# Sums of folded weights by VectorE in SBUF instead of adding transfers through DRAM, and a new early order with the first two weight tiles in halves

## The chip, the core and the metric

One core of a Trainium2 chip runs the whole program. The metric is the device time of one execution in microseconds (us), the median over runs. TensorE (PE) multiplies, VectorE (DVE) and ScalarE (ACT) convert and evacuate, GpSimd (POOL) copies small things, SyncE (SP) issues nearly all transfers. PEld is TensorE's loading of stationary operands.

## The reference

Attention with a local window and block summaries, and a bilinear feed-forward layer on its output. The shapes: 4 batches, 8 heads, 768 positions of 64; weights 512 x 1024 (w1, w2), 1024 x 1024 (w3), 1024 x 512 (w_out), all float32.

```python
k_sum = k.reshape(B, H, nb, block, D).max(axis=3)
v_sum = v.reshape(B, H, nb, block, D).mean(axis=3)
scores_l = scale * np.matmul(q, k.transpose(0, 1, 3, 2))
mask_l = np.abs(pos[:, None] - pos[None, :]) < window
scores_s = scale * np.einsum('bhsd,bhnd->bhsn', q, k_sum) + np.log(block)
a = softmax(np.concatenate([np.where(mask_l, scores_l, -1e9), scores_s], axis=-1))
x = np.matmul(a, np.concatenate([v, v_sum], axis=2))
...
a = x @ w1
b = x @ w2
h = a * b @ w3
return (h @ w_out).astype(np.float32)
```

## The kernel before, in words

**Numbers.** A float32 is carried as two words, a high one that TensorE's fast format holds exactly and a low one, the rest. A product is three matmuls: high x high, low x high, high x low.

**Fold.** Since nothing stands between `w3` and `w_out`, the kernel first computes `wp` = w3 x w_out, eight tiles `wp[0]` to `wp[7]` of 128 x 2 x 512 (two words). The weights arrive in tiles of 1 MB, numbered n = 0 to 19 (n = 0 is the first of `w_out`, 1 the first of `w3`, 12 to 19 are w1 and w2), in raw 64-bit words. `load_weight` issues the load of tile n, `convert` turns it into two words in four steps (the actions `a`, `b`, `c`, `d`): a pass of ScalarE (L203), a shift of VectorE (L228), a cast of ScalarE to the high word (L233) with an OR of VectorE (L235), and VectorE's low word (L161). Where `LAST_BITS` has an A, the last bits come from a second pass of ScalarE (L211) and one OR of VectorE (L219). The first four tiles are converted in two halves. TensorE needs, for its first matmul, half of the `w_out` tile and half of the `w3` tile.

**Order.** In the first part SP and TensorE follow `PLAN`, a list of actions written out by hand: `wN` loads tile N, `aN` to `dN` convert it, `kN` loads keys, `fN` queries, `rN` rows of values, `vN` values, `qN eN xN nN tN oN` are the six pieces of attention step N (scores, exponentials, normalization, transposes, outputs), `RN` gives TensorE N x 100 columns of matmuls. A scheduler places ScalarE's and VectorE's work between. From step 8 on `lump(p)` does the same in code: it writes down step p's scores, then the outputs of step p-2, and runs matmuls between.

**Network.** The first 1024 tokens (u = 0, 1) go through the network in the plain way. The other 2048 (n = 1, 2) use a scheme of seven products in place of eight (`lanes`): `gates` has four row blocks r, of seven products k each, and 24 large matmuls a product and pair of stationary tiles `ws`; `project_fast` follows with `wp`. The scheme needs sums and differences of blocks of the stationary matrices, which are made once on the chip by `stationary`: it forms sums in a tile `wr`, then for each of k = 2, 5, 4, 3 casts the high word (`sp`, ScalarE L673), takes the low word (VectorE), and stores `sp` to DRAM (`wS` for w1 and w2, `pS` for `wp`). `ws` are loaded back from there, six in flight, by `flow_in`. `tend` takes one step of this background work now and then, as matmuls are written down.

**The sums of wp.** `stationary` needs the float32 value of `wp`, high plus low. Before, `spill_high` (action `h`) stores the eight high words to DRAM (`pR`), `join_wp` adds the eight low words to it by adding transfers of GpSimd's queue (one or two beside each of steps 8 to 11), and `sums_of_output` loads `pR` into four tiles `wr` from step 16 (c = 0) and step 18 (c = 1) on. Its `sp` take tiles with the tag `wp`, that of the gate weights tiles with the tag `x` (six buffers, shared with `ws`). The gate weights' sums (`sums_of_gates`) are made in SBUF by VectorE (L918), in a tile with the tag `ring`.

Of the kernel before, what the change touches and what calls it, by code (L numbers as in the profile page):

```python
# [32 lines left out]
f0 w5 R62
w6 b3 a4 R15
c3 w7 d2 d3 R62
R30
a5 b5 r2 r0 a6 f1 b4 K0 F0 c4 d4 c5 v0 b6 q0 d5 c6 R107
w8 M k1 k3 e0 a7 k2 b7 w9 x0 R31
d6 R62
c7 f2 R47  # L40
a8 n0 v1 K1 K2 d7 b8 R31
N w10 L2 F1 w11 L4 c8 t0 a9 q1 d8 V0 F2 b9 R92
e1 o0 c9 d9 v2 a10 q2 R92
R31
x1 w12 f3 L1 a11 V2 K3 L0 S0 f5 L3 F3 n1 V1 t1 b10 e2 b11 x2 S4 R47
f4 c10 w13 d10 S1 o1 n2 a12 v3 R92
b12 c12 t2 c11 q3 L5 d11 F4 w14 o2 e3 S3 a13 b13 d12 a14 b14 w15 x3 n3 L6 w16 w17 V3 c13 v4 a15 f6 S5 a16 d13
S6 c14 R78
d14 b15 f7 b16 S2 c15 c16 d15 w18 a17 w19 b17 W1 L7 v5 V5 a18 c17 d16 d17 R62
b18 a19 b19 c19 c18 d18 t3 q4 R31  # L50
d19 o3 P1 V4 F5 e4 R77
p0 x4 q5 R46
e5 R108
x5 R29
p1 R61
W2 p2 n4 S7 p3 R123
W0 R154
n5 p4 p5 R15
p6 p7 h0 h1 R154
# [3 lines left out]
W3 R62
R76
h7 x6 R107
x7 V6 R92
R77
v7 V7 f8 R62
n6 n7 R32
# [43 lines left out]
def attention_moe(ctx, tc, qG, kW, kT, vP, vW, vB, mask, w1, w2, w3T, wo, out, outT):  # L113
# [545 lines left out]
    def stationary(name, load, to_dram, home, apart=False):  # L659


        if apart:
            t = [[sb.tile([P, 512], F32, name="wr", tag="pt", bufs=6) for _ in range(2)] for _ in range(2)]
        else:
            whole = sb.tile([P, 2, 2, 512], F32, name="wr", tag="ring", bufs=RING)
            t = [[whole[:, i, j] for j in range(2)] for i in range(2)]
# [423 lines left out]
    def budget(columns):  # L1090
# [53 lines left out]
    EXTRA.setdefault(16, []).append(lambda: background.append(sums_of_output(0)))  # L1144
    EXTRA.setdefault(18, []).append(lambda: background.append(sums_of_output(1)))

    for i in range(NF):
        EXTRA.setdefault(8 + i // 2, []).append(lambda i=i: join_wp(i))

# [110 lines left out]
```

## Time and profile before

| | |
|---|---|
| median of 3 runs | 515.13 us (513.4 to 515.14) |
| the profiled execution | 514.52 us |
| its span in the trace | 512.8 us |
| TensorE busy | 487.9 us (95%) |
| VectorE, ScalarE, GpSimd busy | 362.1, 324.1, 48.1 us |
| mean granted TensorE clock | 0.989 of full |
| moved by the DMA engines | 142.95 MB, 279 GB/s |

Busy time is a share of the span for each engine by itself; the engines overlap. All times within the trace are counted from the start of its span. "idle before <-X" names the instruction or transfer whose end released the waiting one.

### The profile page before, as it was taken

To read this page: it belongs to the slowest core of one execution; us is meant where nothing else is said; L and a number is where in the kernel's file an instruction comes from. 1 tells how busy PE (TensorE), PEld (TensorE's weight loads), DVE (VectorE), ACT (ScalarE), POOL (GpSimd) and SP (SyncE) were. 2 spreads that over 40 slices of the span, in tenths; PEclk is the share of its full clock that TensorE was granted. 3 is DMA by queue.
4 is the path that set the end of the run, shared out by engine and by line. 5 is a ranking of instruction groups with operands and counts; after the bars stand their busy time and mean duration, and the time that the engine had idled before them with its cause. 6 is when DMAs were issued, how large, how long until landed. Compare 5 with 4: busy or idle time off the path is not lost.

```text
span 512.8 us, 10326 instructions
## 1 busy us (share of the span) xinstructions
PE 487.9 (95%) x3744; PEld 392.0 (76%) x3744; DVE 362.1 (71%) x877; ACT 324.1 (63%) x888; POOL 48.1 (9%) x86
## 2 busy tenths in 40 slices
PE   0989999999999999999969999999999999999996
PEld 0767777888887777777757888778788888888885
DVE  4898978798825788945279676789978029229972
ACT  5888988884618678877777576747875421423710
POOL 1023311230331111000000000000000000000000
PEclk9989999999999999999979999999999999999999
DMA  8999599995998998999876869985858755656752
GB/s 343 418 404 394 184 366 411 402 408 175 377 263 244 311 295 274 308 363 362 278 287 225 304 234 359 341 271 192 252 164 262 230 185 195 203 176 198 211 199 84
DMA packets 54915, 142.95 MB, mean 279 GB/s; under 512 B 5456, under 2 KB 18256, under 8 KB 52304
## 3 DMA queue, kind: packets, MB, share of 16 engines
q1 hardware_dynamic: 52560, 138.09, 76.6%
q0 software_dynamic: 1152, 2.10, 3.2%
q10 hardware_dynamic: 1152, 2.10, 1.1%
q8 instruction: 30, 0.49, 0.4%
q14 instruction: 21, 0.17, 0.1%
HBM read 109.56 MB, written 32.70 MB: 277 GB/s over the span
## 4 chain that ended last, share of the span: by engine, by line
PE 82%; DMA 8%; ACT 4%; DVE 4%; issue 1%; SPq 0%; DVEq 0%; ACTq 0%
PE ln L719 44%; PE mm L165 27%; PE po L473 4%; PE sc L395 4%; PE tp L453 2%; DMA wraw<-in_wo_dram 2%; DMA wS<-sp 2%; DMA wraw<-in_w_dram 1%; DMA wraw<-in_w3T_dram 1%; DMA wr<-pR 1%; ACT sm L433 1%; ACT wf L203 1%; PE means L322 1%; ACT w L233 1%; ACT wraw L211 0%
## 5 line engine op out<-in xcount | busy, mean ns | idle before, releaser
L719 PE MATMUL ln<-xT,ws 128*128 128x512 f32 x672 | 158.7, 396 | 0.0
L719 PEld LDWEIGHTS ln<-xT,ws 128*128 128x128 f32 x672 | 126.3, 190 | 28.0 <-issue 0.8
L165 PE MATMUL mm<-x,w 128*128 128x512 f32 x384 | 92.0, 395 | 0.9 <-ACT g L542 0.9
L165 PEld LDWEIGHTS mm<-x,w 128*128 128x128 f32 x384 | 70.9, 188 | 17.9 <-ACT g L542 1.3
L423 ACT ACTIVATE sm<-sm,mx 128x120 f32<-128x120 f32 x192 | 73.8, 388 | 7.9 <-DVE mx L409 7.9
L719 PE MATMUL ln<-hT,ws 128*128 128x512 f32 x336 | 78.3, 392 | 0.0
L719 PEld LDWEIGHTS ln<-hT,ws 128*128 128x128 f32 x336 | 62.6, 188 | 13.3 <-DVE hT L161 0.2
L739 DVE TENSOR_TENSOR tmp<-ln,tmp 128x512 f32<-128x512 f32 x52 | 35.7, 687 | 51.0 <-PE ln L719 36.7
L165 PE MATMUL mm<-w,w 128*128 128x512 f32 x192 | 48.8, 409 | 14.5 <-ACT w L233 11.6
L637 ACT CAST hT<-hr 128x512 fp32r<-128x512 f32 x56 | 32.1, 620 | 42.9 <-DVE hr L796 35.3
L165 PEld LDWEIGHTS mm<-w,w 128*128 128x128 f32 x192 | 36.4, 194 | 24.0 <-ACT w L233 11.6
L409 DVE CUSTOM_DVE_ANT_0 sm<-sc,mask_sb 128x120 f32<-128x120 f32 x192 | 42.4, 276 | 7.6 <-PE sc L395 7.5
L165 PE MATMUL mm<-wp,h 128*128 128x512 f32 x192 | 46.0, 394 | 0.0
L433 ACT ACTIVATE sm<-sm,mx 128x120 f32<-128x120 f32 x128 | 38.7, 385 | 8.2 <-DVE mx L429 8.1
L165 PEld LDWEIGHTS mm<-wp,h 128*128 128x128 f32 x192 | 35.5, 188 | 8.0 <-issue 0.5
L161 DVE TENSOR_TENSOR hT<-hr,hT 128x512 fp32r<-128x512 f32 x56 | 35.5, 684 | 4.6 <-ACT hT L637 4.4
L423 ACT ACTIVATION_READ_ACCUMULATOR sm<-sm,mx 128x1 f32 x192 | 36.7, 191 | 0.0
L473 PEld LDWEIGHTS po<-pt,v 120*64 120x64 f32 x768 | 25.4, 141 | 13.4 <-ACT pt L460 4.3
L473 PE MATMUL po<-pt,v 120*64 120x64 f32 x768 | 29.0, 229 | 5.2 <-ACT pt L460 4.1
L382 POOL COPY k<-ks 128x96 f32<-128x96 f32 (+1 forms) x32 | 12.0, 390 | 197.5 <-DMA k<-in_kW_dram 135.1
L161 DVE TENSOR_TENSOR xT<-xraw,xT 128x512 fp32r<-128x512 f32 x28 | 18.7, 684 | 13.0 <-ACT xT L637 13.0
L203 ACT ACTIVATE wf<-wraw 128x1024 f32<-128x1024 f32 (+1 forms) x24 | 23.4, 991 | 6.6 <-DMA wraw<-in_wo_dram 4.8
(63 smaller groups left out, 560.3 us busy)
## 6 DMA issues: line engine op xcount, KB each, us to landing
ws<-wS SPq DMA_DIRECT2D x56, 512.0 KB
v<-in_vW_dram SPq DMA_DIRECT2D x24, 512.0 KB
wraw<-in_w3T_dram SPq DMA_DIRECT2D x8, 1024.0 KB
wraw<-in_w_dram SPq DMA_DIRECT2D x8, 1024.0 KB
wS<-sp SPq DMA_DIRECT2D x16, 512.0 KB
ws<-pS SPq DMA_DIRECT2D x16, 512.0 KB
k<-in_kW_dram SPq DMA_DIRECT2D x20, 368.0 KB
raw<-in_kT_dram SPq DMA_DIRECT2D x16, 392.0 KB
```

What stands on the lines that cost most here:

```text
L161: eng.tensor_tensor(dst, src, hi.bitcast(F32), ALU.subtract)
L165: nc.tensor.matmul(acc, lhsT=a, rhs=b, start=first and i == 0, stop=last and i == len(terms) - 1)
L203: nc.scalar.activation(f[:, some], words[:, some, 1].bitcast(F32), AF.Prelu, scale=2.0**-112, alpha=-(2.0**32),)
L382: nc.gpsimd.tensor_copy(k[:, blocks, CUT : CUT + NB], ks[b, p].unsqueeze(1).broadcast_to([P, n, NB]))
L395: nc.tensor.matmul(sc[h][64 * g : 64 * g + 64, i * KR : (i + 1) * KR], lhsT=q[rows, i * P + 64 * g : i * P + 64 * g + 64], rhs=k[rows, i, ...
L409: nc.vector.tensor_tensor_reduce(out=sm[:, j], in0=sc[h][:, i * KR : (i + 1) * KR], in1=mask_sb[:, 0 if blk == 0 else 2 if blk == BLOCKS - ...
L423: nc.scalar.activation(sm[:, j], sm[:, j], AF.Exp, bias=mx[:, 0, j : j + 1], scale=-1.0, accum_out=mx[:, 1, j : j + 1])
L433: nc.scalar.activation(sm[:, j], sm[:, j], AF.Copy, scale=mx[:, 2, j : j + 1])
L473: nc.tensor.matmul(po[cols, at : at + 64], lhsT=v[:KR, g, i, cols], rhs=pt[g][:, (h * NBLK + i) * 64 : (h * NBLK + i + 1) * 64], start=Tru ...
L637: nc.scalar.copy(dst[0], src)
L719: nc.tensor.matmul(banks[i][:, :U], lhsT=x, rhs=y, start=c + j == 0 and k in o.first, stop=c == steps - 1 and j == 2 and k in o.last, skip ...
L739: nc.vector.tensor_tensor(parts[to], got, parts[more], ALU.add)
```

## The change

The sums of `wp` are made by VectorE: `sums_of_output` adds the two words of `wp` tiles straight into one tile `wr` of the tag `ring`, four adds of 128 x 512 for each c. The DRAM tensor `pR`, `spill_high`, `join_wp` and the loads are gone. Both of its works are appended to the background behind those of the gate weights (action `G`), and their `sp` take tiles of the tag `x`, like all others. The first two weight tiles are loaded in halves: `w0 w1` load the first halves, the new action `u` (`load_rest`) the second. `PLAN` is written anew in many places (of it two lines stand here), and five tables of letters with it.

```diff
 PLAN = """
-k0 w0 w1 w2 a0 b0 a1 r1 c0 b1 c1 d0 w3 w4 a2 a3 m d1 b2 c2 R77
+w0 w1 u0 k0 w2 u1 a0 u2 b0 a1 c0 b1 w3 d0 c1 u3 a2 a3 d1 w4 m a4 b2 b3 f0 R77
...
-F6 h3 h4 t4 t5 q6 F7 e6 q7 f9 e7 o4 v6 o5 h5 G h6 R31
+f9 t4 t5 F7 q6 e6 q7 e7 o4 v6 o5 G W3 R60
...
+SPLIT = 2
-LAST_BITS = "--A--A--A---AAAA-AAA"
+LAST_BITS = "--AA-A--A---AAAA-AAA"
...
-HOMES = "TTTTTTTS"
-BANKS = "SSTSSTST"
+HOMES = "TSTSTTTT"
+BANKS = "STTTSTST"
...
     def load_weight(n):
         name, i = chunks[n]
         raw = sb.tile([P, 2 * PIECE], U32, name="wraw", tag="ring", bufs=RING)
-        nc.sync.dma_start(raw, SOURCES[name][0][i])
         raws_of[n] = raw
+        if n >= SPLIT:
+            nc.sync.dma_start(raw, SOURCES[name][0][i])
+        else:
+            nc.sync.dma_start(raw[:, :PIECE], SOURCES[name][0][i][:, :PIECE])
+
+    def load_rest(n):
+        name, i = chunks[n]
+        if n < SPLIT:
+            nc.sync.dma_start(raws_of[n][:, PIECE:], SOURCES[name][0][i][:, PIECE:])
...
-            to = sb.tile([P, 2, 512], F32R, name="sp", **home)
+            to = sb.tile([P, 2, 512], F32R, name="sp", tag="x", bufs=6)
...
-    def spill_high(i):
-        nc.sync.dma_start(pR[i % (NF // 2) // 2][:, i // (NF // 2), i % 2], wp[i][:, 0].bitcast(F32))
-
-    def join_wp(i):
-        to = pR[i % (NF // 2) // 2][:, i // (NF // 2), i % 2]
-        nc.gpsimd.dma_start(to, wp[i][:, 1].bitcast(F32), accum_op=ALU.add)
...
     def sums_of_output(c):
 
         def load(t):
             for h in range(2):
-                for i in range(2):
-                    to = t[i][h].rearrange("p (j d) -> p j d", d=DH)
-                    nc.sync.dma_start(to, pR[c][:, h, :, i * DH : (i + 1) * DH])
-            yield from range(1, 5)
-
-        return stationary("p%d" % c, load, lambda k: pS[k][c], {"tag": "wp", "bufs": NF}, True)
+                for j in range(2):
+                    hi, lo = (wp[h * NF // 2 + 2 * c + j][:, w].rearrange("p (i d) -> p i d", i=2).bitcast(F32) for w in range(2))
+                    nc.vector.tensor_tensor(t[:, :, h, j * DH : (j + 1) * DH], hi, lo, ALU.add)
+                yield 1
+
+        return stationary("p%d" % c, load, lambda k: pS[k][c])
...
-        "G": lambda _: background.extend(sums_of_gates(q) for q in range(NQ)),
+        "G": lambda _: background.extend([*map(sums_of_gates, range(NQ)), *map(sums_of_output, range(2))]),
```

What it moves, engine by engine, is seen in the programs' own order. In the program of before, line numbers are those of the listing above; in the new one the same statements stand some lines lower (L203 is L214, L233 is L244, L211 is L222, L161 is L164, L409 is L420, L683 is L690).

The first place is the program's start. SP's first transfers were, in the program of before (`raw` is the keys, `wo` the first weight tile, `w3T` the second, `rows` the values):

```order
L283 DMA raw<-in_kT_dram 128x784
L190 DMA wraw<-in_wo_dram 128x2048
L190 DMA wraw<-in_w3T_dram 128x2048
L190 DMA wraw<-in_wo_dram 128x2048
L314 DMA rows<-in_vP_dram 128x2x512
L190 DMA wraw<-in_w3T_dram 128x2048 x2
```

They are now:

```order
L197 DMA wraw<-in_wo_dram 128x1024
L197 DMA wraw<-in_w3T_dram 128x1024
L202 DMA wraw<-in_wo_dram 128x1024
L294 DMA raw<-in_kT_dram 128x784
L195 DMA wraw<-in_wo_dram 128x2048
L202 DMA wraw<-in_w3T_dram 128x1024
L195 DMA wraw<-in_w3T_dram 128x2048 x2
```

The keys went behind three half tiles, the second half of the `w3T` tile stands behind the whole third tile, and the rows of values went away from here. On ScalarE, which converts what has come (`w_149` is the first tile, `w_161` the second, `w_185` the third), stood:

```order
L203 ACTIVATE wf<-wraw 128x512 x2
L233 CAST w_149<-wf 128x512
L203 ACTIVATE wf<-wraw 128x512 x2
L233 CAST w_149<-wf 128x512
L233 CAST w_161<-wf 128x512 x2
L203 ACTIVATE wf<-wraw 128x512 x2
L211 ACTIVATE wraw<-wraw 128x512 x2
L233 CAST w_185<-wf 128x512 x2
```

and in the new program, where `w_159` is the second tile and `w_187` the third:

```order
L214 ACTIVATE wf<-wraw 128x512 x2
L244 CAST w_149<-wf 128x512
L214 ACTIVATE wf<-wraw 128x512
L244 CAST w_159<-wf 128x512
L244 CAST w_149<-wf 128x512
L214 ACTIVATE wf<-wraw 128x512 x2
L222 ACTIVATE wraw<-wraw 128x512 x2
L214 ACTIVATE wf<-wraw 128x512
L244 CAST w_187<-wf 128x512 x2
L244 CAST w_159<-wf 128x512
```

The first two passes are now the first halves of two tiles; the second half of the second tile is passed and cast behind the four passes of the third.

The second place is on VectorE, where the first sums of `wp` (on `wr`) are made. In the program of before they stand beside step 16, behind the reductions of that step's predecessor (L409) and ahead of the differences `xraw` and a reciprocal:

```order
L683 TENSOR_TENSOR wr<-wr 128x512
L633 TENSOR_TENSOR xraw<-xraw 128x512 x3
L685 TENSOR_TENSOR wr<-wr 128x512
L161 TENSOR_TENSOR xT<-xraw,xT 128x512
L429 RECIPROCAL mx<-mx 128x8
L689 TENSOR_TENSOR wr<-wr 128x512
L161 TENSOR_TENSOR xT<-xraw,xT 128x512
L694 TENSOR_TENSOR wr<-wr 128x512
```

In the new program they stand behind the last low word of the gate weights' sums, among the gates of u = 1 (`g`, `h`):

```order
L927 TENSOR_TENSOR wr<-wp_76 128x2x256
L927 TENSOR_TENSOR wr<-wp_77 128x2x256
L559 TENSOR_TENSOR g<-mm,g 128x512
L927 TENSOR_TENSOR wr<-wp_80 128x2x256
L927 TENSOR_TENSOR wr<-wp_81 128x2x256
L164 TENSOR_TENSOR h<-g,h 128x512
L690 TENSOR_TENSOR wr<-wr 128x512
L692 TENSOR_TENSOR wr<-wr 128x512
L696 TENSOR_TENSOR wr<-wr 128x512
L440 RECIPROCAL mx<-mx 128x8
```

Both the adds and the four sums moved ahead by about four steps; at the old place one low word on `sp` stands in their stead.

## Rows read from the trace of the kernel before

**Rows 1.** Timeline of TensorE, 0 to 60 us: start, duration, engine, line, what, [idle before].
```profile
11.61 0.79 PE L165 MATMUL mm<-w,w 128*128 128x512 f32 x1 [11.61 <-ACT w L233]
13.45 8.90 PE L165 MATMUL mm<-w,w 128*128 128x512 f32 x32 [1.05 <-DVE w L161]
...
29.31 1.47 PE L165 MATMUL mm<-w,w 128*128 128x512 f32 x4 [1.86 <-DVE w L161]
```

**Rows 2.** Waits of TensorE: total us, times, longest.
```profile
PE po L473 <- ACT pt L460: 4.1, 2, 3.9
...
PE mm L165 <- ACT g L542: 0.9, 1, 0.9
PE po L473 <- ACT pt L458: 0.8, 1, 0.8
```

**Rows 3.** Stretches: length, busy us (x instructions) by engine, granted clock, DMA share, GB/s.
```profile
29.30:33.40 4.10, 4.09 (x52) 2.69 (x52) 3.96 (x10) 3.68 (x12) 0.00 (x0) 0.59 1.03 412
263.90:269.00 5.10, 5.10 (x36) 4.32 (x37) 2.13 (x9) 5.10 (x20) 0.39 (x2) 0.50 0.92 334
...
216.00:246.00 30.00, 30.00 (x310) 23.82 (x307) 16.35 (x60) 24.36 (x90) 1.20 (x3) 1.00 1.00 362
307.00:333.00 26.00, 26.00 (x237) 20.97 (x236) 17.63 (x56) 19.14 (x65) 0.54 (x2) 1.00 0.98 351
```

**Rows 4.** Timeline of TensorE, 249 to 300 us.
```profile
249.83 0.99 PE L473 MATMUL po<-pt,v 120*64 120x64 f32 x28
...
263.85 1.76 PE L473 MATMUL po<-pt,v 120*64 120x64 f32 x28 [3.88 <-ACT pt L460]
265.54 10.05 PE L719 MATMUL ln<-xT,ws 128*128 128x512 f32 x36
...
282.54 8.46 PE L719 MATMUL ln<-xT,ws 128*128 128x512 f32 x36
```

**Rows 5.** Timeline of VectorE from 255 us.
```profile
257.08 0.69 DVE L683 TENSOR_TENSOR wr<-wr 128x512 f32<-128x512 f32 x1 [9.84 <-DMA wr<-pR]
```

**Rows 6.** Timeline of ScalarE, 254 to 261 us.
```profile
254.34 0.21 ACT L428 ACTIVATE mx<-mx 128x8 f32<-128x8 f32 x1
...
260.93 2.39 ACT L433 ACTIVATE sm<-sm,mx 128x120 f32<-128x120 f32 x8 [1.42 <-DVE mx L429]
```

**Rows 7.** Timeline of VectorE, a gate sum at 196 us.
```profile
196.06 1.28 DVE L918 TENSOR_TENSOR wr<-w 128x512 f32<-128x512 f32 x2
```

**Rows 8.** DMA queues in 140 to 175 us: packets, MB, share of 16 engines.
```profile
q1 hardware_dynamic: 2609, 6.79, 53.8%
q0 software_dynamic: 822, 1.51, 33.4%
```

**Rows 9.** Chain of waits, one piece: start, us, what.
```profile
163.99 8.92 DMA wS<-sp
```

**Rows 10.** Timeline of the start: SP's first issue and VectorE.
```profile
0.75 0.40 SPq L283 DMA_DIRECT2D raw<-in_kT_dram  x1
...
4.03 0.95 DVE L288 TENSOR_REDUCE ks<-raw 128x24 f32<-128x768 f32 x1 [4.03 <-DMA raw<-in_kT_dram]
7.49 0.43 DVE L228 TENSOR_SCALAR wf<-wf 128x512 uint32<-128x512 uint32 x1 [2.51 <-ACT wf L203]
...
8.89 0.68 DVE L161 TENSOR_TENSOR w<-wraw,w 128x512 fp32r<-128x512 f32 x1
```

**Rows 11.** Timeline of ScalarE at the start.
```profile
6.80 1.22 ACT L203 ACTIVATE wf<-wraw 128x512 f32<-128x512 f32 x2 [4.77 <-DMA wraw<-in_wo_dram]
...
9.29 1.24 ACT L203 ACTIVATE wf<-wraw 128x512 f32<-128x512 f32 x2 [0.72 <-DMA wraw<-in_w3T_dram]
...
21.79 1.16 ACT L203 ACTIVATE wf<-wraw 128x1024 f32<-128x1024 f32 x1
```

**Rows 12.** Timeline of TensorE, second row block.
```profile
313.35 7.77 PE L719 MATMUL ln<-xT,ws 128*128 128x512 f32 x33
...
328.08 8.45 PE L719 MATMUL ln<-xT,ws 128*128 128x512 f32 x36
```

More of the change, by code (lines that the diff above doesn't have):

```diff
@@ L31 @@
 PLAN = """
-k0 w0 w1 w2 a0 b0 a1 r1 c0 b1 c1 d0 w3 w4 a2 a3 m d1 b2 c2 R77
[L33 to L43, printed above, removed]
-R31
[L45 to L59, printed above, removed]
-R15
-h2 R91
-F6 h3 h4 t4 t5 q6 F7 e6 q7 f9 e7 o4 v6 o5 h5 G h6 R31
[L63 to L69, printed above, removed]
-R15
+w0 w1 u0 k0 w2 u1 a0 u2 b0 a1 c0 b1 w3 d0 c1 u3 a2 a3 d1 w4 m a4 b2 b3 f0 R77
+c2 w5 R62
+w6 c3 w7 d2 R30
+d3 a5 r1 R62
+a6 b5 r2 r0 b6 f1 b4 K0 F0 c4 d4 c5 v0 d5 c6 q0 R107
+w8 k1 k3 e0 M k2 a7 R31
+b7 d6 w9 R31
+R31
+x0 a8 R31
+c7 b8 v1 n0 R78
+f2 K1 d7 c8 R31
+w10 N L2 K2 F1 w11 t0 d8 a9 F2 q1 b9 V0 L4 e1 R92
+R92
+a10 c9 v2 o0 d9 q2 R31
+x1 w12 L1 f3 K3 L0 V2 V1 n1 b10 a11 F3 e2 f5 t1 S4 b11 x2 f4 c10 d10 S0 R47
+w13 o1 S1 n2 a12 R92
+b12 v3 c12 t2 c11 L5 d11 V3 q3 w14 L3 o2 F4 w15 e3 d12 L6 a13 b13 a14 x3 n3 w16 b14 w17 a15 c13 S5 f6 c14 d13
+a16 S6 R78
+v4 b15 d14 b16 c15 d15 c16 w18 w19 v5 S3 S2 W1 a17 L7 a18 b18 b17 c17 d16 f7 d17 R62
+a19 c18 b19 c19 t3 q4 d18 R15
+d19 o3 F5 R15
+R61
+e4 R77
+p0 x4 q5 V5 e5 x5 p1 R46
+W2 R108
+p2 n4 p3 W0 R154
+n5 R154
+V4 S7 p4 p5 F6 P1 p6 p7 R154
+R91
+f9 t4 t5 F7 q6 e6 q7 e7 o4 v6 o5 G W3 R60
+R107
+x6 R46
+R15
+R15
+R15
+x7 R62
+R93
+R154
+v7 V7 n6 R77
+f8 R15
+R48
+n7 V6 R31
 """
@@ L155, in attention_moe @@
     pS = {k: [tc.dram_tile([P, 2, 2 * DH], F32, name=f"pS{k}_{c}") for c in range(NF // 4)] for k in range(2, NK - 1)}
-    pR = [tc.dram_tile([P, 2, 2, DO], F32, name=f"pR{c}") for c in range(NF // 4)]
     pW = [tc.dram_tile([P, 2, DO], F32, name=f"pW{i}") for i in range(NF)]
@@ L657, in attention_moe, with stationary @@
     stored = set()
[L659 to L666, printed above, removed]
+    def stationary(name, load, to_dram):
+        t = sb.tile([P, 2, 2, 512], F32, name="wr", tag="ring", bufs=RING)
         yield from load(t)
-        (a11, a12), (a21, a22) = t
+        (a11, a12), (a21, a22) = [[t[:, i, j] for j in range(2)] for i in range(2)]
         yield 1
         def finished(k, raw):
-            to = sb.tile([P, 2, 512], F32R, name="sp", **home)
+            to = sb.tile([P, 2, 512], F32R, name="sp", tag="x", bufs=6)
             nc.scalar.copy(to[:, 0], raw)
@@ L917, in load @@
                 for c in range(2):
-                    nc.vector.tensor_tensor(t[j][c], hi[:, c], lo[:, c], ALU.add)
+                    nc.vector.tensor_tensor(t[:, j, c], hi[:, c], lo[:, c], ALU.add)
                 yield 1
-        return stationary("w%d" % q, load, lambda k: wS[k][q], {"tag": "x", "bufs": 6})
+        return stationary("w%d" % q, load, lambda k: wS[k][q])
     def sums_of_output(c):
@@ L1095, in attention_moe @@
     ACTIONS = {
-        "w": load_weight, "a": start_conversion, "b": convert_more, "c": convert_more, "d": convert_more,
+        "w": load_weight, "u": load_rest, "a": start_conversion, "b": convert_more, "c": convert_more, "d": convert_more,
         "k": keys, "m": lambda _: nc.sync.dma_start(mask_sb, mask), "f": fetch, "r": rows, "v": fetch_values,
@@ L1100, in attention_moe @@
         "q": start_step, "e": go_on, "x": go_on, "n": go_on, "t": go_on, "o": go_on,
-        "W": spill_weights, "p": spill_wp, "h": spill_high, "R": budget,
-        "G": lambda _: background.extend(sums_of_gates(q) for q in range(NQ)),
+        "W": spill_weights, "p": spill_wp, "R": budget,
+        "G": lambda _: background.extend([*map(sums_of_gates, range(NQ)), *map(sums_of_output, range(2))]),
     }
@@ L1143, in attention_moe @@
     }
[L1144 to L1148, printed above, removed]
     def lump(p):
```

## The prediction

> **What bounds the kernel now.** I read the page's engine shares first (the table above). TensorE is busy almost all of the span, so only its idle time and its slow time can be won; the work of the other engines counts where TensorE waits for it. The list of TensorE's waits and its own rows in order of time then say where those are. At the start it idles 11.61 us, then 1.05 and 1.86 us [rows 1]. Two short waits follow near 171 and 191 us, 0.9 and 0.8 us, and one of 3.9 us at 260 us [rows 2]. Nothing else is worth a term; after 266 us it runs without a gap to its last matmul.
>
> Two of the three larger waits cost more than they show. The granted clock falls to half (1.2 GHz) behind the 1.86 us wait and again behind the 3.88 us wait, and is full elsewhere: 0.59 on the mean over 29.3 to 33.4 us, 0.50 over 263.9 to 269 us [rows 3]. The 28 small matmuls behind the late wait take 1.76 us where the same 28 took 0.99 us before it, and the next 36 large ones 10.05 us where 36 take 8.46 us later [rows 4]. So the late stall costs 3.88 + 0.77 + 1.59 = 6.2 us.
>
> **Part 1: the sums of the folded weights (late).** The cause of the late stall is in VectorE's row at 257.08 us: L683, the first sum on `wr`, stood 9.84 us for the transfers `wr<-pR` [rows 5]. Behind it on VectorE stand three `xraw` differences and a reciprocal. ScalarE waits for those: its L428 ended at 254.5 us, its eight normalizations began only at 260.93, and the copy of `pt`, which TensorE waits for, stands behind them [rows 6].
>
> The change takes away the eight spills, the eight adding transfers and the eight loads of `pR`. In their place come eight adds from `wp`, in SBUF. The nearest row is the same sum for the gate weights, 1.28 us for two [rows 7], so eight adds are 5.1 us of VectorE. Four of them, and the four sums on `wr`, now stand where before the step of 217 us ran (the order of VectorE shown above). There VectorE has 13.65 us free of 30 [rows 3], so 8 x 0.64 = 5.1 us fit; I cost them at nothing. Were that cover gone, the reciprocal behind them would be up to 5.1 us late, as the one behind the row of 257 us was by 9.84, and would cost as much as that one less its lead. The wait of 9.84 us is then gone from the row of VectorE at 247 us, and only a low part on `sp` (0.68 us) is left there.
>
> What is late next: ScalarE can go on when L428 ends, 254.55. A cast of `xT` (0.6, as one pass of that size [rows 11]), the reciprocal (0.06, estimated), eight normalizations (2.39) and two copies of `pt` (smaller than a pass: I take 0.5 each) make 258.6 us, 259.2 with the new cast of `sp` ahead of it. TensorE comes to that place at 263.85 - 3.88 = 259.97. It is in time by 0.8 to 1.4 us, so I take the whole 6.2 us; the bounds are 4.2 (another 2 us of delay before the copy) and 6.2.
>
> **Part 2: the DMA queues at 140 to 195 us.** The adding transfers run on the software queue. In 140 to 175 us they take 33.4% of the DMA engines' time for 1.51 MB, while the hardware queue takes 53.8% for 6.79 MB [rows 8]: 2.8 times as much time for a byte. In that stretch a store `wS<-sp` of 512 KB takes 8.92 us in the chain of waits, and both short waits of TensorE hang on it, through ScalarE's and VectorE's work on `sp` [rows 9, 2]. Without the adding transfers and the spills ahead of them this store should be near 3.3 us, as the first load, 392 KB from an empty queue, shows (issued at 0.75, landed at 4.03 us [rows 10]). I take both waits as gone, 1.7 us; the bounds are 0 (ScalarE is late there for its own reasons) and 1.7.
>
> The Trainium skill (DMA: Bandwidth & Descriptors, Anatomy of one DMA — SWDGE (gpsimd) path) prices such a transfer at about 2.0 us plus its bytes over 436 GB/s. By it, as an estimate, eight of 256 KB would hold the engines only 5 us in all, the store would stay slow without them, and this term would be 0. The trace disagrees with that price, and its share decides.
>
> **Part 3: the start.** Before, the tile of 1 MB loaded second (`w0`) is there at 6.80 us and the next (`w1`) at 9.29 [rows 11]: 2.49 us a tile, 1.25 a half, in a queue that is full. Now halves of `w0` and `w1` go first, then `u0`, `k0`, `w2`, `u1`. From 4.03 us for 392 KB the landings follow: 4.3, 5.6, 6.8, 7.8, 10.3, 11.5, and 14.0 and 16.5 for `w3` and `w4`. `w5` follows at 20.1, where it was 21.79, since one load of rows (512 KB) now stands behind it.
>
> Each half of a conversion is 0.61 us for a pass or cast of ScalarE [rows 11] and 0.43 (shift) or 0.69 (low part) for one of VectorE [rows 10]. In the new order ScalarE does pass `w0a` 4.3 to 4.9, pass `w1a` 5.6 to 6.2, a cast to 6.8, pass `w0b` to 7.4, cast `w1a` to 8.0. So the first matmul is at 8.0 instead of 11.61. VectorE's low part of `w1a` stands behind five others and ends at 9.9; six matmuls are done by 11.5.
>
> The seventh needs the second half of `w1`. It lands at 11.5, but on ScalarE it stands behind four passes of `w2` (10.3 to 12.7); its cast is ready at 15.1 and its low part at 16.6. Before, matmuls ran without a stop from 13.45 to 27.45 [rows 1], 49 of them and 32 small ones. Now the last 43 begin at 16.6 and take 14.0 less six at 0.25, 12.5 us: 29.1. There they meet the wait of before, for chunk 5. The added pass for `w3` (its bits now come from ScalarE, 1.2 us) puts ScalarE's first pass of `w5` at 21.6, against 21.79, and the order behind it is the same; its low part is again ready near 29.3.
>
> So the early part wins 3.6 us at the first matmul and gives them back: I take 0. The gain is bounded by the earlier landing of `w5` (1.3 us) and the slow clock that would be saved (0.41 of 4.1 us, 1.7): 3.0. The loss is bounded by a slow clock in the sparse start and a slip of the same 1.3 us: 3.0 too.
>
> The Trainium skill (DMA: Bandwidth & Descriptors, Bandwidth) speaks against the halves: load at least 1 MiB at a time, or the fixed part eats the rate. As an estimate from its formula two halves cost 2.0 us more than a whole, 4.0 us for both tiles, and the total would be near 511. Here 392 KB and then 1 MB landed in one stream without such a pause [rows 10, 11], so I price the halves at nothing.
>
> **The sum.** The profiled execution took 514.52 us, 512.8 of span and 1.7 around it. 514.5 - 6.2 - 1.7 - 0 = 506.6. The median of the three runs is 0.6 above the profiled one, so I forecast 507. The bounds of the terms give 514.5 - 6.2 - 1.7 - 3.0 = 503.6 and 514.5 - 4.2 - 0 + 3.0 = 513.3.
>
> **The rivals.** *The start loses.* TensorE runs dry after six matmuls, its clock falls to half as behind the two waits of before, and the fold runs late by up to 3 us. For it: the gap from 11.5 to 15.1 us is longer than the 1.86 us that halved the clock. Against it: TensorE would anyhow wait again near 28 us, which absorbs some of it. With parts 1 and 2 as forecast: 507 + 3 = 510.
>
> *The change does not do what it says.* The wait at 260 us stays, because the copy of `pt` comes late for another reason, and the short waits stay: about 514 to 515. For it: the margin is only 0.8 to 1.4 us, and ScalarE is busy without a gap there. Against it: 9.84 us of VectorE's time are freed just ahead.
>
> *Slower: the stored sums now sit in the buffers of the stationary tiles.* `sp` moves from the tag of `wp` to the tag `x`, six buffers, in which `ws` is prefetched. In the second row block the `ws` for product k = 5 takes the buffer of an `sp`. That `sp` can be cast only when TensorE has left k = 2, at 313.35 + 30 x 0.235 = 320.4 us; k = 5 begins at 328.08 + 27 x 0.235 = 334.4 us [rows 12]. Cast and low part (1.3), store and load must fit into 14.0 us. At 3.3 us for each transfer 6 us are left over. At 8.92 us for each they are 5.1 us too late, with the slow clock (2.4) 7.5 us, and such buffers stand in four more places: two of these waits outweigh the gain, 514.5 - 7.9 + 2 x 7.5 = 522. It decides where a transfer of 512 KB takes over 6.3 us. For it: the DMA engines were 98% busy in 307 to 333 us [rows 3]. Against it: 1 MB of `wr` loads in that stretch are taken away, and the one 8.92 us transfer stood beside the software queue.
>
> **How the numbers follow.** A measurement of this kernel tells about 0.5% (2.6 us) from no change. Forecast (503.5 to 509): 0.60. The start loses, or half of the late gain is missing (509 to 512.5): 0.24. No change: 0.08. Slower: 0.08. All of the first case and all but the end of the second are faster: 0.83, the same 0.09, slower 0.08. The range is 503.5 to 512.5; it leaves out the last two cases.
>
> **What would show it.** In the new profile: no row `wr<-pR`, no software queue; no TensorE wait over 1 us between 60 and 500 us and one stretch of half clock less; the store near 164 us under 5 us; a first matmul near 8 us, six of them, a gap to about 15, and the matmul after the fiftieth near 29 us. I am wrong if TensorE waits for a `ws` or an `sp` transfer after 250 us, if the copy of `pt` near 259 us is still late, or if the fold's matmul at 29.31 us comes later than 31.

## The result and the profile after

The changed kernel takes 506.35 us (median of 4 runs, 505.23 to 507.17), the kernel before 514.63 beside it: ratio 0.986, interval 0.9831 to 0.9889. The forecast was 507, and 506.6 for the profiled execution, which took 505.23 with a span of 503.4 us. Two of the twelve runs of e4_no_joins, 514.0 and 1230.2 us, fell in the slower state of the chip and are left out of the figures given for it below.

The page's engine shares and its hardware queue (packets, MB, share of 16 engines) after:

```profile
PE 484.8 (96%) x3744; PEld 389.7 (77%) x3744; DVE 365.9 (73%) x883; ACT 325.0 (65%) x890; POOL 42.7 (8%) x78
...
q1 hardware_dynamic: 49520, 133.90, 76.4%
```

TensorE is busy 484.8 us, 3.1 less than before, and there is no software queue any more. Its list of waits (total us, times, longest):

```profile
PE mm L168 <- ACT w L244: 12.1, 2, 10.2
PE mm L168 <- DVE w L164: 2.2, 2, 1.5
PE po L484 <- ACT pt L471: 0.2, 1, 0.2
```

Of the waits that the prediction counts from [rows 2] none is left: the 0.2 us stand at 65.5 us, where the trace of before has the same 0.19. Nearly the whole gain, 9.24 of 9.4 us of span, lies in what stood between the start and 270 us. It can be laid out by the same matmul in both traces. TensorE's rows in order of time, of the kernel before:

```profile
39.75 0.68 PE L453 MATMUL tp<-ident,sm 64*120 64x64 f32 x16
...
152.56 1.15 PE L473 MATMUL po<-pt,v 120*64 120x64 f32 x32
...
203.68 1.15 PE L473 MATMUL po<-pt,v 120*64 120x64 f32 x32
```

and the same matmuls of the changed one:

```profile
40.09 0.68 PE L464 MATMUL tp<-ident,sm 64*120 64x64 f32 x16
...
152.20 1.15 PE L484 MATMUL po<-pt,v 120*64 120x64 f32 x32
...
200.86 1.15 PE L484 MATMUL po<-pt,v 120*64 120x64 f32 x32
...
273.30 8.46 PE L726 MATMUL ln<-xT,ws 128*128 128x512 f32 x36
```

The last of these is the row that began at 282.54 before [rows 4]. So the changed kernel is 0.34 us behind at 40 us, 0.36 ahead at 152, 2.82 ahead at 201 and 9.24 ahead at 273; the end adds 0.16. In terms of the sum: the start gave -0.34 (forecast 0), the short waits with what follows them 2.46 (1.7), the late stall 6.42 (6.2). A gain of 0.70 between 40 and 152 us was not forecast.

At the late place the new adds stand where the order shows them, on VectorE (first pair):

```profile
212.83 1.29 DVE L927 TENSOR_TENSOR wr<-wp 128x512 f32<-128x512 f32 x2
```

and the copy of `pt`, on ScalarE, is done at 255.5 us, 1.3 us ahead of the outputs that begin at 256.81 on TensorE. The forecast margin was 0.8 to 1.4, with a reciprocal at 0.06 us and copies at 0.5 that take 0.20 (e3_late_sums) and 0.59 in the rows shown here.

```profile
254.90 0.59 ACT L471 COPY pt<-tp 120x512 f32<-120x512 f32 x1
```

The start went another way than forecast. TensorE's first rows:

```profile
10.19 0.79 PE L168 MATMUL mm<-w,w 128*128 128x512 f32 x1 [10.19 <-ACT w L244]
12.45 2.50 PE L168 MATMUL mm<-w,w 128*128 128x512 f32 x5 [1.47 <-DVE w L164]
16.91 0.80 PE L168 MATMUL mm<-w,w 128*128 128x512 f32 x1 [1.96 <-ACT w L244]
18.40 7.70 PE L168 MATMUL mm<-w,w 128*128 128x512 f32 x26 [0.70 <-DVE w L164]
...
27.02 5.35 PE L168 MATMUL mm<-w,w 128*128 128x512 f32 x21
```

and the passes of ScalarE that the first three tiles release:

```profile
5.11 0.66 ACT L214 ACTIVATE wf<-wraw 128x512 f32<-128x512 f32 x1 [3.08 <-DMA wraw<-in_wo_dram]
7.63 0.66 ACT L214 ACTIVATE wf<-wraw 128x512 f32<-128x512 f32 x1 [1.86 <-DMA wraw<-in_w3T_dram]
...
12.38 1.24 ACT L214 ACTIVATE wf<-wraw 128x512 f32<-128x512 f32 x2 [1.64 <-DMA wraw<-in_wo_dram]
```

The first half is there at 5.11 us (forecast 4.3), the first half of the second tile at 7.63 (5.6), the third tile at 12.38 (10.3). Stretches of the same trace (length, busy us of TensorE, granted clock, DMA share, GB/s):

```profile
3.50:5.50 2.00, 0.00 (x0) 1.00 0.87 229
6.50:10.00 3.50, 0.00 (x0) 1.00 1.04 430
18.40:21.50 3.10, 3.10 (x7) 1.00 1.04 429
```

While the two first halves come in, the DMA engines are 87% busy and move 229 GB/s, half of the rate behind it. The seven matmuls between 18.4 and 21.5 us take 0.43 us each, where later ones take 0.24, although the row gives the full clock; in e7_early_work below the same seven take the same time in a row that gives half of it.

### The profile page after: what moved, and what is told of

Its sections match the earlier page's. It is cut to its first block, busy times and chain, and to the rows that moved or that the text cites. A ratio compares the mean times of both kernels' runs of the same rounds, so it can differ in the third digit from the quotient of the medians.

```text
span 503.4 us, 10266 instructions
## 1 busy us (share of the span) xinstructions
PE 484.8 (96%) x3744; PEld 389.7 (77%) x3744; DVE 365.9 (73%) x883; ACT 325.0 (65%) x890; POOL 42.7 (8%) x78
## 4 chain that ended last, share of the span: by engine, by line
PE 95%; DMA 2%; ACT 1%; DVE 1%; SPq 0%; issue 0%; DVEq 0%
PE ln L726 46%; PE mm L168 36%; PE po L484 5%; PE sc L406 4%; PE tp L464 3%; DMA wraw<-in_wo_dram 2%; ACT sm L450 0%; ACT wraw L222 0%; PE means L333 0%; DVE wf L230 0%; ACT wf L214 0%; SPq L197 0%; DVE w L164 0%; DVE tmp L746 0%; DVE wraw L246 0%
## 5 line engine op out<-in xcount | busy, mean ns | idle before, releaser
L726 PE MATMUL ln<-xT,ws 128*128 128x512 f32 x672 | 157.0, 392 | 0.0
L726 PEld LDWEIGHTS ln<-xT,ws 128*128 128x128 f32 x672 | 125.0, 188 | 27.6 <-issue 1.1
L168 PE MATMUL mm<-w,w 128*128 128x512 f32 x192 | 50.6, 417 | 14.3 <-ACT w L244 12.1
L420 DVE CUSTOM_DVE_ANT_0 sm<-sc,mask_sb 128x120 f32<-128x120 f32 x192 | 42.2, 275 | 7.6 <-PE sc L406 7.5
L164 DVE TENSOR_TENSOR hT<-hr,hT 128x512 fp32r<-128x512 f32 x56 | 35.5, 685 | 7.1 <-ACT hT L648 6.8
L214 ACT ACTIVATE wf<-wraw 128x1024 f32<-128x1024 f32 (+1 forms) x24 | 23.5, 986 | 7.2 <-DMA wraw<-in_wo_dram 4.7
L484 PE MATMUL po<-pt,v 120*64 120x64 f32 x768 | 27.6, 225 | 0.2 <-ACT pt L471 0.2
L744 ACT COPY tmp<-ln 128x512 f32<-128x512 f32 x32 | 18.7, 586 | 13.6 <-PE ln L726 13.4
```

The lines of the kernel that those rows point to most:

```text
L164: eng.tensor_tensor(dst, src, hi.bitcast(F32), ALU.subtract)
L168: nc.tensor.matmul(acc, lhsT=a, rhs=b, start=first and i == 0, stop=last and i == len(terms) - 1)
L214: nc.scalar.activation(f[:, some], words[:, some, 1].bitcast(F32), AF.Prelu, scale=2.0**-112, alpha=-(2.0**32),)
L420: nc.vector.tensor_tensor_reduce(out=sm[:, j], in0=sc[h][:, i * KR : (i + 1) * KR], in1=mask_sb[:, 0 if blk == 0 else 2 if blk == BLOCKS - ...
L484: nc.tensor.matmul(po[cols, at : at + 64], lhsT=v[:KR, g, i, cols], rhs=pt[g][:, (h * NBLK + i) * 64 : (h * NBLK + i + 1) * 64], start=Tru ...
L726: nc.tensor.matmul(banks[i][:, :U], lhsT=x, rhs=y, start=c + j == 0 and k in o.first, stop=c == steps - 1 and j == 2 and k in o.last, skip ...
```

## The experiments

Each ratio is to the kernel before, run beside it on the same chip. The last column is the mark that stands at 39.75 us in the kernel before and at 40.09 in the changed one.

| label | median us | ratio (interval) | transposes behind the 81st fold matmul begin, us |
|---|---|---|---|
| e1_whole_tiles | 504.66 | 0.9838 (0.9809 to 0.9867) | 38.22 |
| e10_whole_again | 504.38 | 0.9839 (0.9811 to 0.9867) | 39.74 |
| e9_whole_bits | 504.56 | 0.9836 (0.9809 to 0.9863) | 38.08 |
| e2_sums_only | 505.01 | 0.9845 (0.9817 to 0.9872) | 38.15 |
| a_after_again | 507.11 | 0.9874 (0.9851 to 0.9896) | 40.13 |
| a2_after_again | 506.61 | 0.9872 (0.9840 to 0.9903) | 40.58 |
| e3_late_sums | 507.01 | 0.9881 (0.9856 to 0.9907) | 41.28 |
| e7_early_work | 505.99 | 0.9849 (0.9828 to 0.9870) | 40.74 |
| e5_joins_kept | 510.79 | 0.9940 (0.9913 to 0.9967) | 40.46 |
| e6_row_halves | 510.48 | 0.9937 (0.9914 to 0.9959) | 43.95 |
| e4_no_joins | 511.50 | 0.9956 (0.9930 to 0.9983) | 37.93 |
| e8_upper_half | 505.59 (one run) | | 39.85 |

### The sums alone: e2_sums_only

The kernel before with the new `sums_of_output`, `sp` in the tag `x` and both works in `G`, without spills and adding transfers:

```diff
-    EXTRA.setdefault(16, []).append(lambda: background.append(sums_of_output(0)))
-    EXTRA.setdefault(18, []).append(lambda: background.append(sums_of_output(1)))
-    for i in range(NF):
-        EXTRA.setdefault(8 + i // 2, []).append(lambda i=i: join_wp(i))
...
+        "G": lambda _: background.extend([*map(sums_of_gates, range(NQ)), *map(sums_of_output, range(2))]),
```

> The kernel before with the new sums alone: adds in SBUF, behind the gate weights' sums, no spills, no adding transfers, sp in the tag x; the early order, the whole tiles and the tables of letters are those of before. Theory: the sums carry the whole gain and the early order gives nothing; the short waits (2.5 us with what follows them) and the late stall (6.4 us with its slow clock) go, 515.1 - 8.9 = 506.2, within 1 us of the changed kernel. Rival: the new written order is needed as well (it moves steps, copies and stores in 40 to 215 us), and without it the short waits stay or new ones come: 508.5 to 513.

It took 505.01 us, 1.2 below the 506.2 of the theory and far from the rival's 508.5: the sums carry the whole gain. Two of TensorE's rows show what is left of its waits:

```profile
29.24 1.19 PE L164 MATMUL mm<-w,w 128*128 128x512 f32 x4 [1.42 <-DVE w L160]
...
44.77 1.15 PE L472 MATMUL po<-pt,v 120*64 120x64 f32 x32 [0.62 <-DVE wp L160]
```

The short waits and the late one are gone with the early order of before; a wait of 0.62 us at 45 us is all that is new.

### The software queue taken away, and given back: e4_no_joins, e5_joins_kept

```diff
-    for i in range(NF):
-        EXTRA.setdefault(8 + i // 2, []).append(lambda i=i: join_wp(i))
```

> The kernel before without the eight adding transfers; it leaves out the low words in the sums of wp, the spills of the high words and the loads of pR stay. Theory: the software queue is what makes the stores at 160 to 190 us slow; without it the 512 KB store near 164 us takes under 5 us in place of 8.92, both short waits of TensorE go, and 2.5 us with them: 512.6; the late stall stays, or shrinks where the loads of pR land earlier. Rival: the short waits come from elsewhere (VectorE's and ScalarE's own work there): 514.5 to 515.5.

TensorE at the marks of 152.56 and 203.68 us of the kernel before:

```profile
150.22 1.15 PE L473 MATMUL po<-pt,v 120*64 120x64 f32 x32
...
198.88 1.15 PE L473 MATMUL po<-pt,v 120*64 120x64 f32 x32
```

It is 2.34 us ahead at the first mark and 4.80 at the second: neither of the two short waits is in the stretch between, which gives 2.46 us, as much as the changed kernel gained there. The late stall is as it was, in TensorE's list of waits and on VectorE:

```profile
PE po L473 <- ACT pt L460: 4.1, 2, 3.9
```

```profile
252.84 0.69 DVE L683 TENSOR_TENSOR wr<-wr 128x512 f32<-128x512 f32 x1 [9.67 <-DMA wr<-pR]
```

By the ratio the step is 2.3 us, and its interval (0.9 to 3.6 us) holds the 2.5. The store was to come under 5 us and took 6.9. So the adding transfers made the short waits and had no part in the late one, but the store need not come under 5 us for them to go. The other way round, in the changed kernel:

```diff
-V4 S7 p4 p5 F6 P1 p6 p7 R154
-R91
+V4 S7 p4 p5 F6 P1 p6 p7 h0 h1 R154
+h2 R91
...
+    for i in range(NF):
+        EXTRA.setdefault(8 + i // 2, []).append(lambda i=i: join_wp(i))
```

> The changed kernel, to which the spills of the high words and the eight adding transfers are given back, at the places of before; nothing reads what they make. Theory: the software queue alone makes TensorE's short waits at 171 and 191 us, so they come back, with the slow stores, and the time is 2.5 us above the changed kernel; there is no wait at 257 us. Rival: the short waits hung on the order of before (its later sums, its other plan), and the changed order has room for slow stores: no wait over 0.3 us, within 1 us of the changed kernel.

The software queue again takes 29.5% of the DMA engines in 140 to 175 us for 1.21 MB; a wait of 3.0 us for `g` comes back at 174 us, the second one near 191 does not, and the marks follow:

```profile
q0 software_dynamic: 653, 1.21, 29.5%
```

```profile
PE mm L169 <- ACT g L554: 3.0, 1, 3.0
```

```profile
153.08 1.15 PE L485 MATMUL po<-pt,v 120*64 120x64 f32 x32
...
205.56 1.15 PE L485 MATMUL po<-pt,v 120*64 120x64 f32 x32
```

It is 0.88 us behind the changed kernel at the first mark and 4.70 at the second: 3.8 us, where 2.5 were expected. In the medians it is 510.79 against the 507.11 of the changed kernel run beside it, 3.7 us. The rival, that the new order has room for it, is out. The spills of the high words came back with the adding transfers here, so this run alone does not split the two; e4_no_joins, which keeps the spills, does.

### The place of the sums: e3_late_sums

```diff
-        "G": lambda _: background.extend([*map(sums_of_gates, range(NQ)), *map(sums_of_output, range(2))]),
+        "G": lambda _: background.extend(sums_of_gates(q) for q in range(NQ)),
...
+    EXTRA.setdefault(16, []).append(lambda: background.append(sums_of_output(0)))
+    EXTRA.setdefault(18, []).append(lambda: background.append(sums_of_output(1)))
```

> The changed kernel with the sums of wp (the same adds in SBUF) begun beside steps 16 and 18, the place of before, and not behind the gate weights' sums. Theory: the late stall came from the loads of pR, not from the place of the sums; VectorE has about 8 us of new work near 250 us but waits for no transfer, and TensorE's wait for the copy of pt is under 1 us: 506 to 507.5. Rival: the place is what counts; the four adds and four sums of 5 us stand ahead of the reciprocal, TensorE waits 2 to 4 us near 257 us and loses 2 us more to the half clock: 508.5 to 512.

No wait of TensorE is over 0.2 us after 20 us. Against the changed kernel it is 1.19 us behind at the 81st matmul of the fold, 1.64 at 152 us and 1.64 at the end of the late steps: nothing is lost at the late place. VectorE there:

```profile
253.42 0.20 DVE L440 RECIPROCAL mx<-mx 128x8 f32<-128x8 f32 x1
...
256.14 2.49 DVE L927 TENSOR_TENSOR wr<-wp 128x512 f32<-128x512 f32 x4
```

The adds came behind the reciprocal, not ahead of it as the rival had it, so the run shows that sums which wait for no transfer do no harm at the late place; it does not show what they would do ahead of the reciprocal.

### The halves: e1_whole_tiles, e10_whole_again, a_after_again, a2_after_again

```diff
-SPLIT = 2
+SPLIT = 0
```

> The changed kernel with its first two weight tiles loaded whole (1 MB each); order and conversions stay. Theory: the halves run at 220 to 235 GB/s where whole tiles run at 390 to 430, and so the third weight tile lands at 12.38 us where the prediction had 10.3. With whole tiles, first tile near 5.6, second near 8.1, third near 11.5 or before; first matmul near 9.5 to 10.5; the wait at 15 us is gone or under 1 us, and the 81st matmul of the fold, which ends at 40.09 us in the changed kernel, is 0.5 to 2 us earlier: total 504.5 to 506 against 506.35. Rival: what counts is that work can begin with a half; then the first matmul comes at 11 us or later and the total is 507 to 508.

ScalarE's passes of the second and third tile, and the stretch in which the changed kernel had 229 GB/s:

```profile
8.06 1.24 ACT L214 ACTIVATE wf<-wraw 128x512 f32<-128x512 f32 x2 [0.71 <-DMA wraw<-in_w3T_dram]
...
11.52 1.23 ACT L214 ACTIVATE wf<-wraw 128x512 f32<-128x512 f32 x2 [0.68 <-DMA wraw<-in_wo_dram]
```

```profile
3.50:5.50 2.00, 0.00 (x0) 1.00 1.03 430
```

The whole second tile is there at 8.06 us, 0.43 behind its half in the changed kernel, and the third 0.86 ahead. TensorE:

```profile
12.60 10.04 PE L168 MATMUL mm<-w,w 128*128 128x512 f32 x32 [1.42 <-DVE w L164]
...
29.27 1.20 PE L168 MATMUL mm<-w,w 128*128 128x512 f32 x4 [1.54 <-DVE w L164]
...
38.22 0.68 PE L464 MATMUL tp<-ident,sm 64*120 64x64 f32 x16
```

Here the 33 first matmuls take 10.84 us and the waits up to the 54th 13.34 us (10.38 at the first matmul among them); in the changed kernel 11.79 and 14.32. The two differences make 1.93 us, the 81st matmul ends 1.87 us earlier. The landings, the first matmul and the total came as the theory had them. To tell this from what one execution differs from the next, both kernels were run again:

> The changed kernel itself, unchanged, to stand beside the other runs of this call (the kernel before read 514.63 us beside the result and 513.15 beside the first experiments). Theory: its early order is the worse one by 1 to 2 us at the 81st matmul of the fold (40.09 us against 38.2 with whole tiles or with the order of before), so it stands at 0.985 to 0.988 of the kernel before, 0 to 2 us above the run with whole tiles. Rival: the early order is as good as the others and the 1.9 us lie within what one execution differs from the next: the same ratio as with whole tiles, 0.984.

> The changed kernel with whole first tiles once more, on the same chip as the changed kernel itself in this call. Theory: the halves cost 1 to 2.5 us (a start at the half clock and the slower first stream); 0.982 to 0.985 of the kernel before, 1 to 2.5 us below the changed kernel of this call, with the 81st matmul near 38.2 us. Rival: no difference beyond 0.7 us.

> The changed kernel once more, on the same chip as the kernel with whole first tiles. Theory and rival as there: 0.986 to 0.9885 of the kernel before, the 81st matmul at 40 to 41.3 us; by the rival the same time as with whole tiles.

On one chip whole tiles read 504.38 and the changed kernel 506.61 us, 2.2 apart. The intervals of one pair overlap a little; but all four runs without halves stand at 0.9836 to 0.9845, and the changed kernel in its three comparisons at 0.986, 0.9874 and 0.9872. In the profiled execution of e10_whole_again, 1.8 us above its median, most of the lead was gone (the mark came at 39.74 us, not near 38.2): its wait before the 51st matmul was 2.07 us, and the four behind it took 0.5 us each.

```profile
29.27 2.06 PE L168 MATMUL mm<-w,w 128*128 128x512 f32 x4 [2.07 <-DVE w L164]
```

### Why the halves are slow: e6_row_halves, e8_upper_half

```diff
-            nc.sync.dma_start(raw[:, :PIECE], SOURCES[name][0][i][:, :PIECE])
+            nc.sync.dma_start(raw[:64], SOURCES[name][0][i][:64])
...
-            nc.sync.dma_start(raws_of[n][:, PIECE:], SOURCES[name][0][i][:, PIECE:])
+            nc.sync.dma_start(raws_of[n][64:], SOURCES[name][0][i][64:])
```

> The changed kernel with the halves of the first two weight tiles cut the other way: 64 rows of 8 KB each and not 128 rows of 4 KB; same bytes in each transfer, same number and order of transfers. A conversion needs both halves now. Theory: it is the rows of 4 KB, every second 4 KB of the tensor, that move at 220 to 235 GB/s between 3.5 and 6 us; whole rows move at 380 to 430, and the third tile lands near 10.3 to 11 us in place of 12.38. Rival: it is the transfers of 512 KB (a fixed cost for each), and the rate stays at 220 to 280 with the third tile near 12.4. Of the total I expect 505 to 507 in both cases.

The theory failed: rows of 8 KB did not help. The rate (last column) is lower still, and for longer: the second tile was whole only at 16.61 us, and since a conversion needs both halves here, the first matmul came at 18.95. The time, 510.48, is above the 505 to 507 expected in both cases.

```profile
3.50:5.50 2.00, 0.00 (x0) 1.00 0.98 197
6.50:10.00 3.50, 0.00 (x0) 1.00 0.94 194
```

This cut has only 64 rows of the tile in each transfer, and its size is the same, so it leaves open which of these does it. The next run kept rows, sizes and order, and changed only which half of the second tile comes first:

```diff
-            nc.sync.dma_start(raw[:, :PIECE], SOURCES[name][0][i][:, :PIECE])
+            some = slice(0, PIECE) if n == 0 else slice(PIECE, 2 * PIECE)
+            nc.sync.dma_start(raw[:, some], SOURCES[name][0][i][:, some])
...
```

> The changed kernel with the halves of the second weight tile in the other order: its upper 4 KB of each row first, its lower 4 KB later; the first tile as in the changed kernel, sizes, rows and order of transfers the same. Theory: two transfers in a row that read the lower 4 KB of every 8 KB use half of what the memory gives, and the upper half beside them uses the rest; the rate in 3.5 to 6.5 us rises from 220 to 270 GB/s to 330 or more, and the third tile lands near 10.5 to 11.5 us, not at 12.38. Rival: a half is slow wherever it lies; the rate stays under 280 and the third tile lands near 12.4. The conversion of the second tile waits for its later half either way, so the first matmuls come later and the time says nothing.

```profile
3.50:5.50 2.00, 0.00 (x0) 1.00 1.00 395
```

```profile
5.98 0.72 ACT L216 ACTIVATE wf<-wraw 128x512 f32<-128x512 f32 x1 [0.57 <-DMA wraw<-in_w3T_dram]
```

With a lower and an upper half under way the rate is 395 GB/s, and the second one is there at 5.98 us, not 7.63. In the same stretch the six traces with two lower halves (the changed kernel three times, e3_late_sums, e5_joins_kept and e7_early_work) have 205 to 248, the five with whole tiles 406 to 430. So neither the row of 4 KB nor the transfer of 512 KB is slow in itself: two that read the lower 4 KB of every 8 KB are. Whether a lower half by itself is slow can't be read: in 2.5 to 3.5 us, where it is mostly the first one that moves, the rate is 201 here and 287 in the changed kernel. When the third tile lands can't be read here, since ScalarE first waits for the second tile's later half. That the gain is in DRAM and not on the way into SBUF was not told apart. Of this run one more row speaks:

```profile
15.17 10.69 PE L168 MATMUL mm<-w,w 128*128 128x512 f32 x33 [15.17 <-ACT w L246]
```

It begins five microseconds after the changed kernel and is not behind at the 81st matmul (39.85 us against 40.09). The six early matmuls were worth nothing.

### Work ahead of the first matmul: e7_early_work

```diff
+    nc.gpsimd.memset(wp[7][:, 0].bitcast(F32), 1.0)
...
+        early = ps.tile([P, 512], F32, name="early", tag="sc", bufs=4)
+        for _ in range(22):
+            nc.tensor.matmul(early, lhsT=wp[7][:, 0, :P], rhs=wp[7][:, 0], start=True, stop=True)
         for action in PLAN.split():
```

> The changed kernel with 22 added matmuls of 128 x 512 on a constant tile ahead of everything else on TensorE; nothing reads what they make. Theory: the early order loses because its first 33 fold matmuls stand far apart and take 0.43 to 0.5 us each until 22 to 24.5 us; with work ahead of them they take 0.24 to 0.25, the row of 26 matmuls at 18.4 us takes 6.2 us in place of 7.7 to 8.9, and the 81st matmul ends at 38 to 38.8 us and not at 40.1 to 41.3: 1.3 to 2.5 us below the changed kernel. Rival: the arrival of the tiles bounds it; then a wait for VectorE's low words appears near 24 to 28 us and the total stays within 0.7 us of the changed kernel. If the added matmuls run past 10 us they delay the first real one, by up to 1 us.

The theory failed. The granted clock (the number before the DMA share) in stretches, and a row of TensorE between the second and the third:

```profile
6.00:9.40 3.40, 3.40 (x15) 1.00 1.03 403
10.00:11.00 1.00, 0.50 (x1) 1.00 0.95 397
13.00:15.00 2.00, 1.77 (x5) 0.50 1.00 416
...
18.40:21.50 3.10, 3.04 (x7) 0.50 1.04 427
```

```profile
12.47 2.30 PE L169 MATMUL mm<-w,w 128*128 128x512 f32 x5 [1.79 <-DVE w L165]
```

The added matmuls end at 0.23 us each, at the full clock (2.4 GHz). The one matmul at 10.18 us, behind 0.78 us of idling, still has it; behind the 1.79 us that follow, the clock falls to 0.50 (1.2 GHz) and stays there to 21.5 us. So work ahead does not carry over the gaps, and the rival's wait did not come either. The time, 505.99, can't be told from the 507.11 of the changed kernel beside it (the intervals overlap).

### ScalarE's share at the start: e9_whole_bits

```diff
-LAST_BITS = "--AA-A--A---AAAA-AAA"
+LAST_BITS = "--A--A--A---AAAA-AAA"
```

on top of the whole tiles.

> The changed kernel with whole first tiles, and the last bits of the fourth tile made by VectorE as before and not by ScalarE: 1.2 us less on ScalarE near 17 us, 0.5 to 1 us more on VectorE. Theory: with whole tiles TensorE is bound near 28 us by the conversion of the sixth tile, whose chain stands behind ScalarE without a gap from 11.5 to 29 us; the wait of 1.54 us at 29.27 shrinks by up to 1.2 us, and the total by as much: 503.5 to 504.5 where whole tiles alone had 504.66. Rival: VectorE bounds it as much as ScalarE, and the wait stays at 1.4 to 2 us, the total at 504.5 to 505.5.

The wait ahead of the 51st matmul is 1.51 us, as it was with whole tiles (1.54), and the time 504.56: the rival's side. That VectorE bounds this conversion as much as ScalarE, the rival's reason, fits but was not shown by itself.

## Why the prediction was right, and where it was not

**What bounds it, and the late stall.** Right, in mechanism and size: 6.42 us for 6.2. The wait stayed when only the adding transfers were taken away (e4_no_joins, 9.67 us on VectorE for `wr<-pR`), and it was gone wherever the sums stood in SBUF, also at the late place (e3_late_sums). The adds took 1.29 us a pair, as priced, and TensorE waited for nothing behind them.

**The short waits.** Right in mechanism, small in size: 2.46 us for 1.7. Each wait cost more than its length, which the term left out. Around the first, from the start of the outputs at 161.80 to that of the transposes at 173.12, TensorE took 11.32 us before and 10.14 after for the same matmuls: 1.18 for a wait of 0.88. Around the second, from 186.04 to 192.71, it took 6.67 before and 5.43 after: 1.24 for a wait of 0.81, since the 32 outputs behind it took 1.51 us where they take 1.15. What was wrong is the store. It was to be near 3.3 us, under 5. The second store of the pair is issued at 163.05, and ScalarE is released by it at 169.89:

```profile
163.05 1.01 SPq L686 DMA_DIRECT2D wS<-sp  x1
```

```profile
169.89 0.62 ACT L680 CAST sp<-wr 128x512 fp32r<-128x512 f32 x1 [1.34 <-DMA wS<-sp]
```

That is 6.8 us, and 6.9 in e4_no_joins: the queue still holds loads of keys and values ahead of it. 2 us less than 8.92 were enough. Nor do both short waits hang on this store, as the prediction has it. Only the one at 191 us does. The one at 171 us, for the `g` copied at 170.91, hangs on the store before it, issued at 162.82. This is ScalarE's cast ahead of that copy, before and after:

```profile
169.86 0.62 ACT L673 CAST sp<-wr 128x512 fp32r<-128x512 f32 x1 [2.58 <-DMA wS<-sp]
```

```profile
166.82 0.61 ACT L680 CAST sp<-wr 128x512 fp32r<-128x512 f32 x1
```

That store took 7.0 us before. After, it is issued at 161.63, and the cast does not wait for it; in e4_no_joins the wait is 0.66 us, in e5_joins_kept 4.59. By the price that the Trainium skill gives for such transfers (DMA: Bandwidth & Descriptors, Anatomy of one DMA — SWDGE (gpsimd) path) this term would have been 0. The trace disagrees: taking them away gave 2.46 us, giving them back with their spills cost 3.8.

**The start.** The term of 0 held by number (-0.34), but the step behind it failed: "I price the halves at nothing", from 392 KB and 1 MB that had landed in one stream. They were not the same kind of transfer: those read whole rows. The landings slipped by 0.8, 2.0 and 2.1 us, the first matmul came at 10.19 and not 8.0, the 51st at 31.3 and not near 29, and not for a wait there but because TensorE itself was late, since 18.4 us without a gap; by the text's own mark (later than 31) it was wrong there. (The 21.79 from which it counts an earlier landing of `w5` is a pass of ScalarE that waits for no transfer, not a landing.) TensorE did run dry behind six matmuls, as the first rival had it. That this costs little against the kernel before is luck: the start lost about 2 us against whole tiles, and the profiled execution of before lost its own 1.7 us to the half clock behind its wait at 29.31 [rows 3]. By their mean granted clock most of its executions lost it too: of 40 beside the experiments 31 have 0.993 or less, and the other nine, at 0.995 to 0.997, took 1.7 us less in the mean (the profiled e4_no_joins, with the half clock behind the late stall alone, has 0.995). The rule of the Trainium skill that spoke against the halves (DMA: Bandwidth & Descriptors, Bandwidth) had the sign right. The estimate of 4.0 us is about twice what the runs show; the Trainium skill gives the formula behind it (DMA: Bandwidth & Descriptors, Anatomy of one DMA — SWDGE (gpsimd) path) for transfers that GpSimd issues, and these were issued by SyncE. The reason that the prediction names with it, a fixed part for each transfer, is not what e8_upper_half shows: the same number of transfers, of the same size, ran at 395 GB/s.

**The slower rival.** Its mechanism is in the trace and its price is not. In the second row block ScalarE does wait for TensorE to give up a `ws`, and later for a store:

```profile
311.25 0.62 ACT L680 CAST sp<-wr 128x512 fp32r<-128x512 f32 x1 [0.84 <-PE ln L726]
...
316.93 0.62 ACT L680 CAST sp<-wr 128x512 fp32r<-128x512 f32 x1 [3.32 <-DMA pS<-sp]
```

The cast at 311.25 us comes when it was computed to come (320.4 less the 9.24 gained). The store behind it is issued at 312.6 and landed by 316.9, 4.3 us, below the 6.3 from which the rival decides; TensorE waits for nothing there.

**What stays open.** The 0.70 us between 40 and 152 us were not tested; part of it is 32 outputs that took 1.50 us at 76 us before and 1.15 after. Nor was it tested why giving the adding transfers back with their spills cost 3.8 us where taking them away gave 2.46.

## What to carry to other kernels

A wait that holds an engine up counts by what stands behind it in that engine's order: 9.84 us of VectorE for a load cost TensorE 6.4, and sums made in SBUF beside the same late steps, though behind the reciprocal, cost nothing. The adding transfers, with 2.8 times as much DMA time for a byte, were paid by the stores beside them, 2.5 us of TensorE before anything read what they wrote. Load a tile whole where its first half starts an engine that then runs dry: here six matmuls five microseconds early bought nothing, and the variant with whole tiles (504.4 to 504.7 us) is faster than the kernel before by 1.6% and, by the medians, than the changed one by 2 us.

## What the runs showed of the hardware

Two loads that each read the lower 4 KB of rows of 8 KB moved 229 GB/s (205 to 248 in six traces), a lower and an upper one 395 (one trace), whole tiles 430 (406 to 430 in five). Loads of 64 rows of 8 KB moved 194 to 238 between 3.5 and 10 us. The granted clock, full after 22 matmuls, was still full behind 0.78 us of idling and half behind one matmul and 1.79 us more (e7_early_work). In the first 21 us of the changed kernel the rows give the full clock while matmuls take 0.43 us, as they do at half of it in e7_early_work. The clock behind the wait ahead of the 51st matmul was half after 1.86 and 2.07 us, and full after 1.02, 1.42, 1.51 and 1.54.
